# Two norms back to back, and the x tiles of batch 0 prepared ahead of the first H matmul

## The chip, the cores and the metric

One core of one Trainium2 chip runs the whole kernel. Times are device microseconds of one execution. A kernel has several runs; I quote medians, and ratios as said in the section on the result. Times in the trace count from the start of the profiled span, which is some 2 us shorter than the run's time. Engines: TensorE (PE; its weight loads are PEld), VectorE (DVE), ScalarE (ACT), GpSimd (POOL), SyncE (SP).

## The reference

Linear attention with elu + 1 as feature map, then a two-layer MLP with a swish of one beta per hidden unit.

```python
def phi(x): return np.where(x > 0, x, np.exp(x) - 1.0) + 1.0
kv  = einsum('bhsd,bhse->bhde', phi(k), v)            # 8 batches, 8 heads, 576 rows, 64
num = einsum('bhsd,bhde->bhse', phi(q), kv)
den = einsum('bhsd,bhd->bhs', phi(q), phi(k).sum(2)) + 1e-6
x   = (num / den) as rows of 512                      # 4608 rows
h   = x @ w_in                                        # 512 x 2048
out = (h * sigmoid(beta * h)) @ w_out                 # 2048 x 512
```

## The kernel before

The kernel works in bf16, one batch after the other. While TensorE computes H and Y of batch b, the other engines prepare batch b + 1. Batch 0 has nothing to hide behind. Its inputs are loaded in pieces, and its first two x tiles (128 rows each) are brought to TensorE one by one:

```python
warm(10); beta_trans(); warm(15)      # matmuls on zeros, to bring TensorE's clock up
... # exp9, relu9, phi9: features of k and of the first part of q; kv; q transposes
num_mm(0, 0)                          # numerator and denominator of x tiles 0 and 1 (PE)
num_mm(0, 1)
num_norm(0, 0)                        # den, reciprocal, multiply -> xs (DVE)
exp9(0, QF, N9)                       # features of the rest of q (ACT, DVE)
relu9(0, QF, N9)
silu_table()                          # dummy Silu: loads the Silu table (ACT)
warm(4)
x_trans(0, 0, dve=True)               # 4 PE transposes, copy from PSUM to SBUF
num_norm(0, 1)
phi9(0, QF, 6)
phi9(0, 6, N9)
...
h_phase(0, xT[0], [(ff, 0, 1) for ff in range(4)] + [(ff, 1, 2) for ff in range(4)] + ...,
        {1: [F(x_trans, 0, 1)],       # after H group 1
         3: [F(q_rest)], ... })       # q_rest: transposes of the rest of q
```

The order of the text is the order of each engine's own instructions. Later, at some 37 to 43 us, batch 1's features are computed while TensorE is in Y of batch 0:

```python
exp_(1, 1); exp_(1, 0); silu_table()  # ACT
relu(1, 1); relu(1, 0)                # DVE
w_out_scale(2)                        # DVE: scales the third w_out block, once its DMA has landed
phi(1, 1)                             # k
phi(1, 0)                             # q; then TensorE transposes q (q_trans, line 395)
```

## Time and profile before

| | before |
|---|---|
| median of the first 3 runs | 292.67 us (292.13 to 292.94) |
| profiled run | 292.05 us, span 290.1, mean granted clock 0.994 |
| TensorE busy | 281.8 us, 97% of the span |
| first H matmul (H0) | 17.09 us |
| dense run of H matmuls from | 22.27 us |
| second phi of batch 1 ends | 42.69 us |
| first q transpose of batch 1 | 42.86 us |

By the *dense run* I mean the 52 H matmuls that follow the last small step of batch 0; in the timeline it is one row ("x52"). From its start the trace shows no idle of TensorE until the q transposes of batch 1.

### The profile page before, as it was taken

The numbers are of one execution on the slowest core, as the hardware profiler recorded it, in microseconds if no ns is written. First come the engines' busy times: TensorE is split into PE (matmuls) and PEld (weight loads), VectorE is DVE, ScalarE is ACT, GpSimd is POOL, SyncE is SP. The second block draws the span as 40 slices with busy tenths as digits, with TensorE's granted clock in tenths as the row PEclk, the third lists the DMA queues.
The fourth block names the chain that finished last, engine by engine and source line by source line (L and its number), as shares of the span: only waits on it lengthen the run. The fifth ranks groups of instructions, "written<-read, shape, count | busy, mean of one in ns | idle before, by whom it ended". The sixth has DMA issues, their size and how long they took to land.

```text
span 290.1 us, 4739 instructions
## 1 busy us (share of the span) xinstructions
PE 281.8 (97%) x1895; PEld 144.1 (50%) x1895; DVE 116.7 (40%) x235; ACT 174.0 (60%) x232; POOL 54.3 (19%) x79
## 2 busy tenths in 40 slices
PE   8889999999999999999999999999999999999994
PEld 3567445644576444454444444554455444444443
DVE  3784487504670365326532654163517300110021
ACT  2788798889998843875277617771750086018500
POOL 8924564400051205020402040000000000000000
PEclk9799999999999999999999999999999999999999
DMA  8999999999379956977894879433503500120033
GB/s 143 196 206 345 254 281 194 257 167 158 62 208 180 136 140 106 196 103 162 121 211 53 161 92 197 77 103 107 97 2 90 111 36 0 72 76 0 0 74 73
DMA packets 75766, 38.07 MB, mean 131 GB/s; under 512 B 43344, under 2 KB 70240, under 8 KB 75744
## 3 DMA queue, kind: packets, MB, share of 16 engines
q0 software_dynamic: 38912, 20.19, 49.0%
q1 hardware_dynamic: 36640, 17.44, 25.7%
q8 instruction: 15, 0.25, 0.4%
q10 hardware_dynamic: 192, 0.14, 0.2%
q14 instruction: 7, 0.06, 0.1%
HBM read 36.71 MB, written 9.44 MB: 159 GB/s over the span
## 4 chain that ended last, share of the span: by engine, by line
PE 92%; DMA 3%; POOL 3%; ACT 1%; issue 0%; DVE 0%; POOLq 0%
PE mm L527 42%; PE mm L475 41%; PE att L421 3%; DMA w_in<-in_moe_w_in_dram 3%; PE att L475 2%; PE att L362 2%; POOL xqk L135 1%; PE mm L559 1%; POOL vraw L135 1%; ACT q_pT L387 1%; PE mm L455 0%; PE att L395 0%; PE att L455 0%; DVE xT L385 0%; DVE y_sb L385 0%
## 5 line engine op out<-in xcount | busy, mean ns | idle before, releaser
L467 ACT ACTIVATE g<-mm,beta_c 128x512 bf16<-128x512 f32 (+2 forms) x160 | 97.8, 623 | 87.1 <-PE mm L475 87.0
L527 PE MATMUL mm<-w_out,g 128*128 128x512 bf16 x560 | 128.0, 379 | 0.0
L475 PE MATMUL mm<-xT,w_in 128*128 128x512 bf16 (+2 forms) x576 | 107.6, 344 | 1.3 <-DMA w_in<-in_moe_w_in_dram 1.2
L475 PEld LDWEIGHTS <-w_in 128*128 128x128 bf16 x672 | 63.8, 98 | 60.8 <-DMA w_in<-in_moe_w_in_dram 1.3
L527 PEld LDWEIGHTS <-g 128*128 128x128 bf16 x560 | 53.1, 98 | 59.0 <-issue 0.3
L537 DVE COPY y_sb<-mm 128x512 f32<-128x512 f32 x27 | 18.7, 692 | 72.9 <-PE mm L527 69.4
L229 ACT ACTIVATE e<-xqk 128x2560 bf16<-128x2560 bf16 x14 | 31.9, 2328 | 0.1
L242 DVE TENSOR_TENSOR qk_p<-r,e 128x2560 bf16<-128x2560 bf16 x14 | 20.8, 1491 | 12.8 <-ACT e L229 12.1
L437 DVE TENSOR_TENSOR xs<-att,rden 128x512 bf16<-128x512 f32 x36 | 24.9, 691 | 1.2
L372 DVE CAST kv_bd<-att 64x260 bf16<-64x260 f32 x14 | 6.0, 427 | 36.6 <-PE att L362 36.5
L435 DVE TENSOR_SCALAR den<-att 128x8 f32<-128x8 f32 x36 | 5.9, 163 | 26.8 <-PE att L421 26.8
L421 PEld LDWEIGHTS <-q_pT 128*128 128x128 bf16 (+1 forms) x160 | 11.1, 102 | 9.5 <-issue 1.3
L421 PE MATMUL att<-kv_bd,q_pT 128*128 128x130 bf16 (+1 forms) x160 | 14.8, 226 | 0.4 <-ACT q_pT L387 0.3
L475 PE MATMUL mm<-xT_tail,w_in 128*128 128x512 bf16 x64 | 14.0, 379 | 0.0
L595 POOL COPY held<-xT 1x1 bf16<-1x1 bf16 x4 | 2.0, 509 | 63.6 <-DMA xT<-xs 63.6
L237 DVE TENSOR_SCALAR r<-xqk 128x2560 bf16<-128x2560 bf16 x14 | 11.9, 853 | 4.0 <-DMA xqk<-in_q_dram 2.5
L612 PE MATMUL mm<-g 128*128 128x512 bf16 x30 | 9.3, 464 | 1.2 <-DVE g L145 1.2
L229 ACT ACT_TABLE_LOAD x7 | 9.0, 1283 | 0.1
L72 POOL DMA_DIRECT2D vraw<-in_v_dram x7 | 6.4, 909 | 10.1 <-DVE vaug L385 4.2
L72 POOL DMA_DIRECT2D xqk<-in_q_dram x7 | 7.1, 1021 | 3.9 <-ACT w_out L214 2.1
L436 DVE RECIPROCAL rden<-den 128x8 f32<-128x8 f32 x36 | 7.3, 203 | 1.2
L72 POOL DMA_DIRECT2D xqk<-in_k_dram x7 | 6.5, 935 | 5.3 <-DMA w_in<-in_moe_w_in_dram 2.5
(77 smaller groups left out, 138.1 us busy)
## 6 DMA issues: line engine op xcount, KB each, us to landing
out_dram<-y_sb SPq DMA_DIRECT2D x28, 256.0 KB, 2.4
xqk<-in_k_dram POOLq DMA_DIRECT2D x7, 512.0 KB, 9.0
xqk<-in_q_dram POOLq DMA_DIRECT2D x7, 512.0 KB, 10.7
vraw<-in_v_dram POOLq DMA_DIRECT2D x7, 512.0 KB, 12.2
w_in<-in_moe_w_in_dram POOLq DMA_DIRECT2D x4, 512.0 KB, 10.1
g<-in_moe_w_out_dram POOLq DMA_DIRECT2D x4, 512.0 KB, 10.9
out_dram<-y_sb SPq DMA_DIRECT2D x14, 128.0 KB, 5.2
xqk<-in_moe_w_out_dram POOLq DMA_DIRECT2D x2, 512.0 KB, 13.7
```

What stands on the lines that cost most here:

```text
L72: eng.dma_start(out=dst[:, :, 0:NJ, :].rearrange("p h j d -> p h (j d)"), in_=src[b, :, 0:MAIN, :].rearrange("h (p j) d -> p h (j d)", j=NJ),)
L229: nc.scalar.activation(st[b, "e", a][:, h0:h1], xqk[b % NX][:, a, h0:h1], ACTF.Exp)
L237: nc.vector.tensor_scalar(st[b, "r", a][:, h0:h1], xqk[b % NX][:, a, h0:h1], 0.0, 1.0, ALU.max, ALU.add)
L242: nc.vector.tensor_tensor(st[b, "p"][:, a].rearrange("p j (h d) -> p h j d", h=H)[:, h0:h1], st[b, "r", a][:, h0:h1], st[b, "e", a][:, h0: ...
L421: nc.tensor.matmul(nps[r0 : r0 + n, p // 2, c0 : c0 + 2 * (D + 1)], st[bb, "qT"][:, t, p, :n], kv_bd[bb % 2][:, p], start=True, stop=True, ...
L436: nc.vector.reciprocal(rden[:n], den[:n])
L437: nc.vector.tensor_mul(xs[:n], nv[:, :, :, 0:D], rden[:n, :, :, None].to_broadcast([n, 2, 4, D]))
L467: nc.scalar.activation(g_sb[b % 2][:, ff, c0:c1], hp[:, c0:c1], ACTF.Silu, scale=beta_c[:, ff : ff + 1],)
L475: nc.tensor.matmul(hp[:, c0:c1], w_in_sb[ff // 4][:, kc, (ff % 4) * P : (ff % 4 + 1) * P], x[:, t0:t1, kc, :] if b < B else x[:, kc, c0:c1 ...
L527: nc.tensor.matmul(yp, g_sb[b % 2][:, ff, t * P : (t + 1) * P], w_out_sb[ff // 4][:, ff % 4, :], start=(ff == 0), stop=(ff == FC - 1),)
L537: nc.vector.tensor_copy(y_sb, yp)
L612: nc.tensor.matmul(st["warm"], g_sb[0][:, FC - 1, 0:P], g_sb[0][:, FC - 1, :], start=True, stop=True, skip_group_check=True,)
```

## The change

The intent is to use the wait for the first weights. VectorE makes both norms in a row. ScalarE, which still holds the Exp table, copies the first x tile out before it loads the Silu table. TensorE transposes the second x tile ahead of H0 instead of between the H groups.

```diff
     num_norm(0, 0)
+    num_norm(0, 1)
     exp9(0, QF, N9)
     relu9(0, QF, N9)
+    warm(4)
+    x_trans(0, 0)
     silu_table()
-    warm(4)
-    x_trans(0, 0, dve=True)
-    num_norm(0, 1)
+    x_trans(0, 1, dve=True)
     phi9(0, QF, 6)
...
         {
-            1: [F(x_trans, 0, 1)],
             3: [F(q_rest)],
```

## The prediction

> **What bounds the kernel now.** I read the page's shares first, then the chain that ended last in order of time, then the timeline of the first 45 us, because every edited line runs there.
>
> The page says that the whole is a TensorE program:
>
> ```profile
> PE 281.8 (97%) x1895; PEld 144.1 (50%) x1895; DVE 116.7 (40%) x235; ACT 174.0 (60%) x232; POOL 54.3 (19%) x79
> PE 92%; DMA 3%; POOL 3%; ACT 1%; issue 0%; DVE 0%; POOLq 0%
> ```
>
> Only 8% of the chain is not TensorE, and nearly all of that is the load of the first weights. VectorE and ScalarE, whose work the change moves, hold about 1%. So the change can act only by letting TensorE's instructions in batch 0 start earlier or waste less. The chain in order of time (start, length, what) shows where:
>
> ```profile
> 9.03 8.02 DMA w_in<-in_moe_w_in_dram
> 17.05 0.05 issue
> 17.09 0.62 PE mm L475 x8
> 17.71 0.22 PE mm L455 x4
> 17.94 0.45 PE mm L475 x8
> 18.38 0.40 PE att L293 x20
> ...
> 33.53 9.50 PE mm L527 x44
> 43.02 0.91 PE att L395 x16
> 43.95 1.95 ACT q_pT L387 x2
> ```
>
> The first H matmul (line 475) starts when the first w_in block lands, at 17.05 us, not when the first x tile is ready. The four transposes of the second x tile (line 455) then cost the chain 0.22 us between the H groups, and the rest of q is transposed (line 293) at 18.38. The timeline (start, length, engine, what, count, idle before and its releaser) gives the x tile's side:
>
> ```profile
> 14.41 0.69 DVE L437 TENSOR_TENSOR xs<-att,rden 128x512 bf16<-128x512 f32 x1
> 15.14 1.28 ACT L618 ACT_TABLE_LOAD   x1
> 15.53 0.39 PE L455 MATMUL mm<-identity,xs 128*128 128x128 bf16 x4
> 15.96 0.42 DVE L385 COPY xT<-mm 128x512 bf16<-128x512 bf16 x1 [0.46 <-PE mm L455]
> 17.09 0.62 PE L475 MATMUL mm<-xT,w_in 128*128 128x128 bf16 x8 [1.17 <-DMA w_in<-in_moe_w_in_dram]
> 17.53 0.63 ACT L467 ACTIVATE g<-mm,beta_c 128x128 bf16<-128x128 f32 x2 [0.89 <-PE mm L475]
> 18.04 0.60 ACT L387 ACTIVATE xT<-mm 128x512 bf16<-128x512 bf16 x1
> ```
>
> The x tile is in place at 16.38; TensorE was idle for 1.17 us and ended that idle on the weights. ScalarE had its Silu table at 16.42 and also waited.
>
> One later place decides what an early gain is worth. These are timeline lines around 39 to 43 us:
>
> ```profile
> 38.99 0.90 DVE L212 TENSOR_SCALAR w_out<-g,rbeta 128x512 bf16<-128x512 f32 x2 [0.19 <-DMA g<-in_moe_w_out_dram]
> 39.81 2.88 DVE L242 TENSOR_TENSOR qk_p<-r,e 128x2560 bf16<-128x2560 bf16 x2
> 42.74 1.00 PEld L395 LDWEIGHTS <-qk_p 128*128 128x128 bf16 x16 [0.21 <-DVE qk_p L242]
> ```
>
> Batch 1's q transposes (line 395) need VectorE's second phi, which ends at 39.81 + 2.88 = 42.69. VectorE gets there from a DMA: the third w_out block lands about 38.97, its scaling takes 0.90, and the two phi follow without a gap. The weight load waited 0.21 us for phi and started at 42.74, hidden under the last Y matmul, so the matmul row (42.86) shows no idle. TensorE and the DMA-VectorE path therefore arrive together here, with some 0.1 us between them at most.
>
> **What the Trainium skill says.** "ScalarE: Activation LUTs", section "Table sets: the hidden batching unit", says that cheap functions, copy among them, are in every table set; so the x copy can run under the Exp table with no third load, and the compiled order shows copy, table load, dummy Silu. The same page, "What ACT_TABLE_LOAD costs", gives about 1283 ns for the load and about 1380 ns more for a drain. The trace has the load at 1.28 us, but no drain: it starts 0.02 us after the Exp and the dummy follows 0.01 us after it. I use the trace. "DMA: Bandwidth & Descriptors", section "Anatomy of one DMA — SWDGE (gpsimd) path", says that waits happen on the issuing sequencer and the DMA engines just consume their queues. The trace agrees in that GpSimd's next issue (17.34) follows the landing of w_in at 17.05. The edit changes neither that order nor those waits. "TensorE: Matmul & The Clock Gate", section "Wait — 56ns, not 53.3ns?", gives 55 to 56 ns between warm 128-column matmuls; here four transposes cost 0.22 us, 55 ns each.
>
> **The change part by part.** No instruction is added or removed; the compiled orders of GpSimd and SyncE are the same.
>
> *Norms back to back.* The second xs followed the first x copy and ended at 16.73 + 0.69 = 17.42. Now it follows the first xs: with the spacing of the first (den to reciprocal 0.21, to multiply 0.23, multiply 0.69) and a start about 15.02, it ends about 16.15. The relu of 0.48 us comes after it, to about 16.55.
>
> *First x copy on ScalarE.* Transposes still end at 15.92 (same norm, same four warm matmuls). The copy takes 15.96 to 16.56 (0.60, as the ScalarE copy at 18.04) instead of VectorE's 16.38. It is 0.18 later but still 0.5 before the weights: free.
>
> *Silu table after it.* 16.58 + 1.28 = 17.86, dummy 0.20, first Silu about 18.0 instead of 17.53. But the 0.60 copy that stood between the second and third Silu is gone. Four Silus at 0.26 spacing then end about 18.0 + 3 x 0.26 + 0.36 = 19.14, against 18.52 + 0.64 = 19.16 now. ScalarE comes out even.
>
> *Second x tile ahead of H0.* Transposes about 16.21 to 16.60, inside the wait for weights; VectorE's copy 16.64 to 17.06; the two phi of the rest follow, about 16.97 to 17.86 (0.88 together), against 18.22 now. On TensorE, 16 H matmuls run from 17.09 to about 18.00 (16 x 0.057), where L293 now starts at 18.32. That is a gain of **0.3 us**: 0.22 of transposes and about 0.1 of handing over. The banks agree: in both kernels, from the third H group on, the four-bank rotation is the same, and the fifth group needs the first Silu's end, about 18.35, when TensorE is ready at about 18.4.
>
> *What reaches the end.* The rest of q goes through VectorE copies (18.82 now) and a ScalarE copy held by them (19.67), so the 0.3 us moves through to the dense H run at 22.95, and to Y at 33.53. Weights do not stop it: GpSimd's waits put the second w_in block's landing before 19.24, and it is first used at 20.37. At 42.7 TensorE would ask for phi 0.3 us earlier. Phi stays where the DMA put it, so the weight load should again start near 42.74 and the first transpose at 42.86. From there on, every start is as before. Sum: 0.3 gained at 18 us, 0.3 waited at 42.7, about **0.0 to 0.1 us net**.
>
> **The rivals.** (a) *The gain survives*: 292.67 - 0.3 = 292.35. For it: the matmul row shows no idle at 42.86, and DMA landings could shift a little. Against it: the weight load already waited 0.21 there. (b) *The late Silu table becomes the bound*: the first Silu is 0.47 later, and if the fifth H group waits for its bank, up to 0.3 is lost: at most 293.0 if nothing later hides it. Against it: the four Silus end together with now, and the same phi wait would absorb a loss of no more than a few hundredths only, so this one would show. (c) *The norms in a row were the bound*, as the intent suggests, and the first x tile matters: worth 0.7 us (17.09 to about 16.4) to 292.0. The DMA releaser of the 1.17 us idle speaks against it.
>
> **Range and chances.** The three runs before span 292.13 to 292.94, more than any of these effects. I centre at 292.67 less half a tenth, pulled slightly towards (a): 292.55. Half the spread of the runs plus (a) below and a mild (b) above give 291.9 to 293.1. Two per cent is 5.9 us, twenty times the largest term; chances: faster 0.01, same 0.98, slower 0.01.
>
> **What would show it.** In the new profile: first H matmul still released by w_in near 17.1; the second x transposes before it; line 293 starting near 18.0; first Silu near 18.0; phi of batch 1 still ending near 42.7 after a DMA-released w_out scaling, and TensorE's weight load of line 395 waiting about 0.5 us instead of 0.21. I am wrong if H0 starts well before the weights did here, if a wait on ScalarE appears before the fifth H group, or if line 395 starts earlier by the 0.3 us.

## The result

The changed kernel took 291.63 us (291.48 to 291.80, 4 runs), the kernel before beside it 292.81 us (292.13 to 293.19, 4 runs). The ratio is 0.9963 with a 95% interval of 0.9943 to 0.9982. A ratio is the mean time of one kernel's fast runs over that of the other's of the same rounds, so not quite the ratio of the medians quoted. This is inside 2%, as predicted, but 291.63 lies below my range (291.9 to 293.1), and 1.2 us between the medians is far more than the 0.1 us that I had given the change.

The profile after, first the page's shares:

```profile
PE 280.2 (97%) x1875; PEld 143.2 (49%) x1895; DVE 116.4 (40%) x235; ACT 174.3 (60%) x232; POOL 54.7 (19%) x79
PE 83%; DMA 9%; POOL 4%; DVE 1%; issue 1%; ACT 1%; POOLq 0%; DVEq 0%
```

The busy times hardly moved. (TensorE has 1.6 us and 20 instructions less than before; the weight loads are still 1895, so the 20 are most likely records missing from the trace.) The chain did: DMA went from 3% to 9% of it. The chain in order of time shows where:

```profile
12.21 15.10 DMA xqk<-in_moe_w_out_dram
27.31 0.28 issue
27.59 11.02 DMA g<-in_moe_w_out_dram
...
39.04 0.79 DVE w_out L212
39.83 2.81 DVE qk_p L242 x2
42.64 0.05 issue
42.68 1.08 PE att L395 x16
43.79 1.95 ACT q_pT L387 x2
```

Before, everything from 17 to 43 us ran through H and Y on TensorE, but for one copy on VectorE. Now nothing of that is in the chain: it is two w_out loads, one scaling, the two phi of batch 1, and then TensorE's q transposes. The timeline of the changed kernel shows the x tiles and the wait at the end:

```profile
13.48 0.69 DVE L437 TENSOR_TENSOR xs<-att,rden 128x512 bf16<-128x512 f32 x1
14.52 0.69 DVE L437 TENSOR_TENSOR xs<-att,rden 128x512 bf16<-128x512 f32 x1
14.77 0.60 ACT L387 ACTIVATE xT<-mm 128x512 bf16<-128x512 bf16 x1 [0.31 <-PE mm L455]
15.26 0.40 PE L455 MATMUL mm<-identity,xs 128*128 128x128 bf16 x4 [0.53 <-DVE xs L437]
15.38 1.28 ACT L618 ACT_TABLE_LOAD   x1
16.73 1.07 PE L475 MATMUL mm<-xT,w_in 128*128 128x128 bf16 x16 [1.07 <-DMA w_in<-in_moe_w_in_dram]
17.73 0.47 PE L293 MATMUL att<-identity,qk_p 64*128 64x64 bf16 x20
42.68 0.90 PEld L395 LDWEIGHTS <-qk_p 128*128 128x128 bf16 x16 [0.74 <-DVE qk_p L242]
42.68 1.07 PE L395 MATMUL att<-identity,qk_p 128*128 128x128 bf16 x16 [0.25 <-DVE qk_p L242]
```

The 16 H matmuls now run in one piece. The rest of q is transposed at 17.73 instead of 18.32, and the dense run starts at 21.68 instead of 22.27: **0.59 us earlier**. Of that, 0.36 is the first weights landing earlier (16.73 against 17.09), which I take for chance: nothing ahead of that load was edited, and its issue already began at 8.57 instead of 9.03. The other 0.23 is the change's: 4.95 us from H0 to the dense run instead of 5.18. At 42.68 the weight load waits 0.74 us for phi, and the transposes start only 0.18 us earlier than before, of which 0.06 is phi itself ending earlier (42.63 against 42.69). The two profiled runs differ by 0.25 us (292.05 and 291.80). So the trace pair shows the absorption that I had predicted, and most of the 1.2 us between the medians is in runs that were not profiled.

The opening of the two traces differs also in what no edit touched: the clock. Windows of 1 us (stretch, length, then busy time of PE, PEld, DVE, ACT and POOL, granted clock, DMA share, GB/s), before, then after:

```profile
13.00:14.00 1.00, 0.94 (x5) 0.33 (x4) 0.32 (x2) 0.96 (x4) 1.00 (x2) 0.50 1.24 208
```

```profile
13.00:14.00 1.00, 0.72 (x7) 0.53 (x8) 0.89 (x3) 0.99 (x2) 1.00 (x2) 1.00 1.23 206
```

Before ran at half clock from about 11.5 to 14.9 us while it computed the first x tile; after did not.

### The profile page after: what moved, and what is told of

The parts are those of the page before. It is cut to its first block, busy times and chain, and to the rows that moved or that the text cites. A ratio compares the mean times of both kernels' runs of the same rounds, so it can differ in the third digit from the quotient of the medians.

```text
span 289.9 us, 4720 instructions
## 1 busy us (share of the span) xinstructions
PE 280.2 (97%) x1875; PEld 143.2 (49%) x1895; DVE 116.4 (40%) x235; ACT 174.3 (60%) x232; POOL 54.7 (19%) x79
## 4 chain that ended last, share of the span: by engine, by line
PE 83%; DMA 9%; POOL 4%; DVE 1%; issue 1%; ACT 1%; POOLq 0%; DVEq 0%
PE mm L527 38%; PE mm L475 37%; DMA xqk<-in_moe_w_out_dram 5%; DMA g<-in_moe_w_out_dram 4%; PE att L421 3%; PE att L362 2%; POOL xqk L135 1%; PE mm L559 1%; PE att L475 1%; POOL w_in L162 1%; DVE qk_p L242 1%; POOL vraw L135 1%; ACT q_pT L387 1%; PE att L395 0%; DVE w_out L212 0%
## 5 line engine op out<-in xcount | busy, mean ns | idle before, releaser
L537 DVE COPY y_sb<-mm 128x512 f32<-128x512 f32 x27 | 18.7, 691 | 72.9 <-PE mm L527 69.4
L72 POOL DMA_DIRECT2D xqk<-in_k_dram x7 | 7.2, 1029 | 5.5 <-DMA w_in<-in_moe_w_in_dram 2.6
```

The source lines that it names most:

```text
L72: eng.dma_start(out=dst[:, :, 0:NJ, :].rearrange("p h j d -> p h (j d)"), in_=src[b, :, 0:MAIN, :].rearrange("h (p j) d -> p h (j d)", j=NJ),)
L537: nc.vector.tensor_copy(y_sb, yp)
```

## The experiments

Two theories to begin with. A: the change is worth little and the runs of before were slow by chance (clock, start-up transfers). B: the change is worth 1.1 us. All runs gave correct results. "Clock" is the mean granted clock of a run.

### The two kernels again, and phi moved

a1 and a2 are the two kernels unchanged. a3 (changed kernel) and a4 (kernel before) take phi off its place behind the scaling:

```diff
-    w_out_scale(2)
+    w_out_scale(2, 4, 0, 2)     # first half of the block
     phi(1, 1)
+    w_out_scale(2, 4, 2, 4)     # second half
     phi(1, 0)
```

> The kernel before, unchanged, as a control: it shows the span and the granted clock of each of its runs, which were not listed with the result. Theory A (the part of the gain that I did not predict comes from TensorE's clock or from the start-up transfers, in the runs of before alone): these runs spread by about 1 us, and the slower ones have a lower granted clock (0.994 or less) or a later first phi. Theory B (the change is worth 1.1 us by its own waits): these runs are at 292.6 to 292.8 with the same clock as the changed kernel, 0.997 to 1.000. Ratio to before expected 1.000 within 0.002 either way.

> The changed kernel, unchanged, with more rounds beside the control. If the 1.1 us are of the change, the ratio is again 0.996 (291.6 against 292.8). If they were chance in four runs each, it is 0.998 to 1.000. The profile should again show the line 395 weight load waiting for phi, 0.5 us or more.

> The changed kernel, with batch 1's first phi put between the two halves of the third w_out scaling. Theory of absorption: phi's second half ends near 42.0 instead of 42.64, the wait of TensorE's weight load of line 395 (0.74 us in the changed kernel) falls to 0.2 or nothing, and the time falls by another 0.2 to 0.4 us, to about 291.3. Rival (the wait is not what holds TensorE there, or another wait takes its place): time as the changed kernel within 0.1.

> The kernel before with the same reorder of phi. TensorE comes to line 395 without slack there, so an earlier phi (by 0.1 to 0.2) gives at most 0.1 us: ratio to before 1.000 within 0.0005. If phi were the bound of before too, it would gain as much as in the changed kernel, 0.2 to 0.4.

| | median (range) | ratio to before, 95% |
|---|---|---|
| before, beside them | 291.80 (291.63 to 292.72, 9 runs) | |
| a1 before | 292.03 (291.79 to 293.91) | 1.0006 (0.9992 to 1.0020) |
| a2 changed | 291.88 (291.84 to 292.22) | 1.0004 (0.9991 to 1.0016) |
| a3 changed, early phi | 291.16 (291.03 to 291.53) | 0.9980 (0.9967 to 0.9992) |
| a4 before, early phi | 291.92 (291.16 to 292.34) | 0.9999 (0.9986 to 1.0012) |

Theory B fell: on this chip the changed kernel is no faster than before, and the same kernel before has runs at 291.63 and at 293.91. The absorption held: with phi out of the way, the changed kernel gains 0.7 us, and the kernel before 0.1, within its noise. The profiled pair shows 0.33 of the 0.7 (291.84 and 291.51; the first q transpose at 42.75 and 42.40), which is what I had expected; the rest is in runs that were not profiled. In a3 the chain again runs through TensorE, and the transposes follow Y directly:

```profile
34.20 8.37 PE mm L527 x38
42.57 0.91 PE att L395 x16
```

a1's profiled run was the slowest of all runs of the kernel before, 293.91 us. Lines of its timeline, and below them one of its windows:

```profile
17.64 0.42 DVE L385 COPY xT<-mm 128x512 bf16<-128x512 bf16 x1 [1.30 <-PE mm L455]
18.11 0.86 PE L475 MATMUL mm<-xT,w_in 128*128 128x128 bf16 x8 [0.51 <-DVE xT L385]
18.41 0.69 DVE L437 TENSOR_TENSOR xs<-att,rden 128x512 bf16<-128x512 f32 x1
19.16 0.40 PE L455 MATMUL mm<-identity,xs 128*128 128x128 bf16 x4 [0.18 <-DVE xs L437]
```

```profile
16.00:18.00 2.00, 1.60 (x7) 0.77 (x6) 0.70 (x3) 1.46 (x2) 0.90 (x1) 0.50 1.25 204
```

Here H0 is not released by the weights but by VectorE's copy of the x tile, and then one thing follows the other: copy, second norm, second transposes. The clock is at half from 11.9 to 18.7 us, and the first Exp, which starts when k has landed, came at 8.22 us instead of 7.78. The prediction had the x tile "0.5 before the weights: free"; in this run it is on the path.

a2's profile shows my rival (b) as real: its clock was halved from 12.3 to 15.7 us, the x copy came at 16.21, the table load behind it, and TensorE waited for the first Silu:

```profile
16.82 1.28 ACT L618 ACT_TABLE_LOAD   x1
18.23 1.12 ACT L467 ACTIVATE g<-mm,beta_c 128x128 bf16<-128x128 f32 x4
18.63 0.58 PE L475 MATMUL mm<-xT,w_in 128*128 128x128 bf16 x7 [0.32 <-ACT g L467]
```

The 0.32 us vanished in the phi wait, which was still 0.43.

### Parts of the change, and a cold start

b1 and b2 split the change, both with the early phi so that a gain is not absorbed. b1 puts the table load back ahead of the copies; b2 moves only the copy:

```diff
# b1, from a3                        # b2, from a4
+    silu_table()                    -    silu_table()
     warm(4)                              warm(4)
-    x_trans(0, 0)                   -    x_trans(0, 0, dve=True)
-    silu_table()                    +    x_trans(0, 0)
+    x_trans(0, 0, dve=True)         +    silu_table()
     x_trans(0, 1, dve=True)              num_norm(0, 1)
```

b3 and b4 are the kernel before and the changed kernel with `warm(1)` in place of both `warm(10)` and `warm(15)`.

> The changed kernel with the early phi, but the first x copy on VectorE and the Silu table where it was before: only the back-to-back norms and the transposes ahead of H0 are left of the change. Theory (the gain at TensorE is the 0.22 us of transposes and the earlier phi of the rest, not ScalarE's copy): median as the changed kernel with early phi, 291.2 within 0.2, and first Silu near 17.0 instead of 17.2. Rival (the copy on ScalarE carries the gain): back to 291.9.

> The kernel before with the early phi, plus only the first x copy on ScalarE ahead of the Silu table; second norm and second transposes where they were. Theory: no gain, median 291.9 within 0.3, as before with the early phi; the Silu table ends later, so H groups may wait for a Silu, up to 0.3 us worse. Rival (the copy carries the gain): 291.2.

> The kernel before with 2 of the 25 opening warm-up matmuls, so that TensorE's clock is surely low in the first 15 us or so. Theory (the runs of before that are slow are those in which the clock is halved while the x path runs, and the change takes transposes and VectorE work out of that path): about 293 to 294.5, granted clock under 0.985, and the first H matmul released by the x copy instead of the weights.

> The changed kernel with the same 2 warm-up matmuls. Theory: it loses less than before does under the same clock, so the ratio between the two is 0.996 to 0.998, 0.6 to 1.2 us. Rival (the clock hits both alike): the two cold kernels are within 0.3 us of each other.

Before had 292.47 here (291.70 to 293.32, 11 runs, in two groups: 291.70 to 291.90 and, but for one at 292.47, 293.07 to 293.32). b1: 291.53 (291.15 to 292.00), ratio 0.9965 (0.9943 to 0.9987). b2: 292.58 (291.83 to 293.05), ratio 0.9996 (0.9973 to 1.0020). The two intervals touch, but only one run of b1 lies above the lowest of b2. So what is left in b1, norms in a row and transposes ahead, carries the gain; the copy on ScalarE alone shows none. In b1's profile the dense run even starts 5.44 us after the first x copy (17.02, on VectorE; 22.46), where the whole change has 5.85 to 6.06 in the table below: in runs in which the x copy comes late, ScalarE's copy with the table load behind it cost some 0.4 us by this one trace. So b1 may be a better version than a3; the two were not run side by side.

b3: 292.79, but from 291.73 to 296.04. b4 (median of all six runs): 291.83, its fast runs 291.54 to 292.55 and one run at 296.55. That points the way I had expected, but the intervals (0.9981 to 1.0068 and 0.9952 to 1.0008) overlap, so it shows little. My sign for a cold start, a clock under 0.985, was wrong: the recorded mean was 0.998 and 1.000, though 128x512 matmuls in b3's opening took 0.61 to 0.63 us instead of 0.38. The mean leaves out the cold start.

### More warm-up, and another chip

d1 (before) and d2 (changed) have `warm(21)` for `warm(15)`; d3 is the changed kernel; d4 is a3 with `warm(21)`.

> The kernel before with 21 instead of 15 warm-up matmuls in the second group, which fill TensorE's wait for the first phi (8.75 to 9.97 us in its first profile). Clock theory (the slow runs of before, 293 us and above, are those in which the clock is halved for one or two stretches of 3.4 us between 11 and 19 us, after that wait): every run at a clock of 0.997 or more, 291.6 to 292.1, no run above 292.5. Rival (start-up transfers make the spread): spread as before, 291.7 to 293.3, at full clock.

> The changed kernel with the same 21 warm-up matmuls. If the change is worth nothing at full clock, because phi absorbs its lead, the median is within 0.2 us of the kernel before with 21; if it has a gain of its own, 0.4 us or more below it.

> The changed kernel on another chip, beside the kernel before. Clock theory: it stays at 291.5 to 292.2 whatever the clock does, while the runs of before split into 291.7 to 292.1 at full clock and 292 to 293.3 at a lower one, so the ratio lies between 0.996 and 1.000 as the chip's runs fall. If it also shows runs above 292.5, the change does not protect against the lower clock.

> The changed kernel with the early phi and 21 warm-up matmuls, as the version that should beat both: 291.0 to 291.3, spread under 0.4. Rival (the added matmuls hold back the first real ones by up to 0.6 us where phi comes early): 291.4 or more.

Before had 292.04 (291.66 to 293.04, 11 runs). d1: 292.30 (291.55 to 293.66), with runs of 292.54 and 293.00 at a clock of 1.000: a low recorded mean does not mark all slow runs. (After b3, a recorded 1.000 does not exclude a slow stretch either.) d2: 291.72 (291.67 to 291.80), ratio 0.9984 (0.9969 to 0.9998). d3: 291.80 (291.62 to 292.11), ratio 0.9986 (0.9970 to 1.0003). d4: 291.52, no better than a3's 291.16 on its chip and what my rival had said; ratio 0.9976 (0.9960 to 0.9991). In d1's profiled run, a fast one, H0 began at 15.82, again released by the x copy, so the weights had landed before then.

### A known delay of the x path

Next theory: before has no slack on its x path and the changed kernel has. A VectorE memset of 704 (e1, e2) or 1408 (e3, e4) elements sits in batch 0's first norm; it took 0.65 and 1.23 us.

```diff
         nc.vector.reciprocal(rden[:n], den[:n])
+        if b == 0 and t == 0:
+            nc.vector.memset(pad, 0.0)
```

> The kernel before with a VectorE memset of some 0.7 us put into batch 0's first norm: a known delay of the x path alone. Slack theory (before has next to no slack between the second xs and its transposes, 0.08 us, and what is lost there reaches the end except what the phi wait takes up): the median rises by 0.4 to 0.7 us above the unpadded kernel before, to 292.4 or more. Rival (the x path is not on the path of before, weights and phi are): within 0.2 us of the unpadded one.

> The changed kernel with the same 0.7 us. Slack theory (first and second x tile have 0.8 us or more to spare there): no change, 291.7 to 291.9, spread under 0.6. Rival: as much more as before has.

> The kernel before with a memset of some 1.4 us. Slack theory: another 0.7 us above the first pad, about 293.1, nearly one for one. Rival: under 292.3.

> The changed kernel with 1.4 us. Slack theory: 0.8 us are taken up ahead of H and about 0.6 at the phi wait, so 291.8 to 292.2; the H groups should now wait for x, and the wait for phi of line 395 shrink from 0.74 to 0.1 or nothing. Rival: one for one as before, 293 or more.

Before had 292.04 (11 runs). Before with the pads: 292.03 and 293.61; changed: 292.06 and 293.37. Most of this contradicts the theory: the first pad cost before nothing, and the second cost the changed kernel almost as much as before. In e1's profile the short pad was hidden: the four warm-up matmuls ran until 15.79, the padded xs ended at 15.70, and TensorE's matmuls show no wait for it. The long one showed. In e4 TensorE stood idle 1.42 us for the padded norm, and then ran its 16 H matmuls at half speed:

```profile
16.04 0.40 PE L458 MATMUL mm<-identity,xs 128*128 128x128 bf16 x4 [1.42 <-DVE xs L440]
17.30 1.87 PE L478 MATMUL mm<-xT,w_in 128*128 128x128 bf16 x16
```

They take 1.87 us instead of 1.07. Here the pad is not a pure delay. The clock was low in nearly every run of e3 and e4 (0.980 to 0.994, one at 1.000); that the idle time lowered it is an inference, and in e3's profile the half clock lay ahead of the wait for the padded norm (12.5 to 15.9, the transposes at 16.23). So the pads can't show slack by themselves.

### A shorter warm-up

f1 (before) and f2 (changed) have `warm(9)` for `warm(15)`.

> The kernel before with 9 instead of 15 matmuls in the second warm-up group: TensorE is idle 1.3 us longer ahead of the first phi, so that the clock should be lowered in most runs. Clock theory: most runs at a clock under 0.997 and a median of 292.4 or more. Rival (the clock of the opening does not matter): 291.9 as at full clock.

> The changed kernel with the same 9 matmuls. Clock theory with the lead of 0.6 us ahead of phi as a reserve: median 291.8 to 292.1, 0.4 us or more below the other. Rival (the lower clock takes as much from both): within 0.2 us of the other.

f1: 291.97 (291.67 to 292.97), ratio 1.0005 (0.9986 to 1.0023). f2: 292.33 (291.61 to 292.59), ratio 1.0001 (0.9985 to 1.0018). The clock was under 0.997 in 11 of the 12 runs, as wanted, and yet f1 did not rise and f2 was not better. "A low mean clock makes before slow, and the change is a reserve against it" fell too, in this form: the mean does not tell which runs are slow.

### What all the profiles have in common

| profile | order | first x copy starts | H0, released by | dense run from | second phi ends | first q transpose | run |
|---|---|---|---|---|---|---|---|
| before | before | 15.96 | 17.09, weights | 22.27 | 42.69 | 42.86 | 292.05 |
| a1 | before | 17.64 | 18.11, x copy | 23.88 | 43.84 | 44.47 | 293.91 |
| d1 | before | 15.34 | 15.82, x copy | 21.59 | 42.40 | 42.46 | 291.55 |
| e1 | before | 16.19 | 16.67, x copy | 22.43 | 42.39 | 43.02 | 292.14 |
| f1 | before | 15.61 | 16.08, x copy | 21.85 | 42.52 | 42.57 | 291.67 |
| after | changed | 14.77 | 16.73, weights | 21.68 | 42.63 | 42.68 | 291.80 |
| a2 | changed | 16.21 | 16.86, x copy | 22.06 | 42.69 | 42.75 | 291.84 |
| d3 | changed | 15.19 | 16.84, weights | 21.79 | 42.67 | 42.72 | 291.85 |
| f2 | changed | 15.53 | 16.18, no idle | 21.38 | 42.46 | 42.52 | 291.61 |
| a3 | changed, early phi | 15.17 | 16.86, weights | 21.81 | 41.89 | 42.40 | 291.51 |

Three regularities follow.

1. The run's time is the first q transpose plus 249.1 us: 248.95 to 249.44 in all 20 profiles, 15 of them within 0.05. Little after that point differs.
2. The first q transpose comes at the later of two times: the dense run's start + 20.59 (a1: 23.88 + 20.59 = 44.47; a3: 21.81 + 20.59 = 42.40), or 0.05 after the second phi (after: 42.63 + 0.05 = 42.68).
3. With the order of before and the first copy on VectorE (8 profiles), the dense run starts 6.24 to 6.31 us after the first x copy, always, also where the idle ahead of H0 ended on the weights. In 7 of the 8, H0 was released by that copy (e1, e3 and b3 have a pad or a cold start ahead of it; d1 and f1 have an earlier copy than before's, a1 and a4 an untouched opening). With the changed order it starts 4.95 us after H0 where the weights released it, or 5.85 to 6.06 us after the x copy where that came late at full speed (a2, f2, b4, d4).

So the change shortens the x path by 0.2 to 0.4 us (6.25 against 5.85 to 6.06). The phi of batch 1, at 42.4 to 42.7, is a floor that both kernels reach with phi in its place: about 249.1 + 42.7 = 291.8 us. It is no fixed time: in a1 it ended at 43.84, because the second phi there waited 0.73 us for ScalarE's Exp, and TensorE came later still.

## Why the prediction was wrong

**Right: the size at H.** I gave 0.3 us (0.22 of transposes and 0.1 of handing over); the change's own part was 0.23 in the first pair of traces and 0.2 to 0.4 in the later ones.

**Right: absorption at phi.** Predicted a wait of about 0.5 us at line 395, measured 0.74, with phi still ending at 42.63 (predicted near 42.7). a3 against a4 is the test: with phi early, 291.16 against 291.92; with phi in its place, 291.88 against 292.03. My net of 0.0 to 0.1 is what this pair allows: before's transposes were bound by TensorE at 42.86, and phi would have let them start at 42.74, so 0.12 was to be had.

**Wrong: "The DMA releaser of the 1.17 us idle speaks against it", in rival (c).** From one trace I took the weights for the bound of H0 and the x tile for free. The second half of the x path, which my own text timed, left no room. Lines of before's timeline:

```profile
16.73 0.69 DVE L437 TENSOR_TENSOR xs<-att,rden 128x512 bf16<-128x512 f32 x1
17.33 0.88 DVE L280 TENSOR_TENSOR qk_p<-r,e 128x512 bf16<-128x512 bf16 x2
17.50 0.27 PEld L455 LDWEIGHTS <-xs 128*128 128x128 bf16 x4
18.31 0.35 PEld L293 LDWEIGHTS <-qk_p 64*128 64x128 bf16 x20
```

The second xs ended at 17.42, its transposes were loaded at 17.50; the rest's phi ended at 18.21, its transposes were loaded at 18.31. That the weights released H0 cost this run no more than 0.07 us (6.31 after the x copy instead of 6.24). In the other seven profiles of that order, the x copy released H0. Both paths were the bound, and the one through VectorE varies: its first copy starts anywhere from 15.34 to 17.64 without a pad, with the landing of k (first Exp at 7.24 to 8.22) and with stretches of half clock. Rival (c)'s reason was right, though not its 0.7 us.

**Wrong: the range, "centre at 292.67".** I took the median of three runs for the level of the kernel and added effects to it. On the four chips of the later runs the kernel before had 49 runs with a median of 292.03, from 291.54 to 293.91. The first job's runs were from its slower part. The term that was mis-sized is the level, by some 0.6 us; the change's own size, as the traces show it, was not. In hindsight, a range from the floor of both kernels up, 291.5 to 293, would have held the result.

**Small slips of the text.** 292.67 - 0.3 is 292.37, not 292.35. The 8% of the chain outside TensorE is not nearly all the first weights: they are the 3% of DMA, and another 3% is GpSimd, mostly issuing the loads of k, q and v. The first Silu came at 17.17 instead of near 18.0, because the whole opening came earlier (first x transposes at 14.35, in before at 15.53). And the wait on ScalarE ahead of the fifth H group, named as a sign of being wrong, did come in a2, with 0.32 us.

In the profiles, the change did 0.2 to 0.4 us in runs bound by TensorE and nothing in runs bound by phi. In the two later comparisons of the same two kernels (a2 and d3), the ratios were 1.0004 and 0.9986, and each interval contains 1. Of the 1.2 us of the result, most therefore lies in slow runs of before.

**Left open.** I can't say what made the first four runs of before slow: they were listed without their clocks, and the profiled run is a fifth. Over the 49 runs, those with a mean clock of 0.997 or more averaged 291.88 (25 runs) and the others 292.57 (24), but d1 was slow at a recorded full clock and f1 fast at a low one, so the recorded clock tells at most part of it. The changed kernel had no run above 292.22 in its 15 without an added pad or changed warm-up, or in the 6 of d2. Of the 59 runs of before that stand beside these (49, the first four, d1), 24 lie above it, with some on every chip. The bound was picked after the fact, but this is hardly luck: the change seems to cut the slow runs of before. The 0.2 to 0.4 us of the profiles are too little for that (before's slowest run was 293.91), and with a pad or a shorter warm-up the changed kernel has runs of 292.5 too (e2, f2). So the cause of the larger part of the 1.2 us is not shown.

**Faster than both:** on its chip, the changed kernel with the early phi (a3), 0.9980 (0.9967 to 0.9992) of before, 291.16 us.

## What to carry to other kernels

When a profile says that an idle ended on a DMA, check how long before that the other inputs were ready along the whole path, not only at its first step: where two paths end within 0.1 us of each other, either can be the bound, and one trace shows only the one that came last in that run. Follow a saved fraction to the next place where TensorE meets another engine; here a phi that waited for a transfer 20 us later took it. Moving that phi gave the kernel before next to nothing (a4) and the changed kernel 0.2 to 0.7 us (d4 against d2, a3 against a2). And take the level and spread of the kernel before from more than three runs before predicting to a tenth of a per cent.

## What the Trainium skill lacked or had wrong

- "ScalarE: Activation LUTs", section "What ACT_TABLE_LOAD costs": it adds a drain of about 1380 ns to each switch. In the changed kernel the load starts at 15.38, 0.01 us after the copy ahead of it ends (14.77 + 0.60), takes 1.28 us, and the dummy Silu starts at 16.68: 0.02 us later. No such drain is seen around it.
- "TensorE: Matmul & The Clock Gate", section "HAM oscillation — how this bites in real kernels": its rule is no idle gaps above about 3.4 us. Before's trace has a half-clock stretch of 3.4 us (11.5 to 14.9) with no idle near that length ahead of it: from the first matmul on the longest was 1.22 us, followed by 2-column matmuls. So keeping to that rule was not enough here. That the idle or the small matmuls caused the stretch is an inference.
- "TensorE: Matmul & The Clock Gate" warns in general that a trace's clock events can be unreliable, but no page says that a mean granted clock can leave out a cold start: b3's was 0.998 while its 128x512 matmuls took 0.61 to 0.63 us in the opening.
